# Layer-norm roots on GpSimd and a tile-by-tile opening in a fused attention and SwiGLU kernel

## The chip, the cores and the metric

The kernel runs on one core of a Trainium2 chip. The metric is the device time of one execution in microseconds; it was measured in three runs. The engines are TensorE (PE, with its weight loads as PEld), VectorE (DVE), ScalarE (ACT), GpSimd (POOL) and SyncE (SP, which here only issues transfers).

## What is computed

```
xn = layernorm(x)                                  # x: 2048 x 640, bf16
q  = (xn @ wq) in 32 heads of 192                  # wq: 640 x 6144
p  = softmax(q k^T / sqrt(192))                    # k, v: 32 heads x 2048 x 192
s  = (p v, heads side by side) @ wo                # wo: 6144 x 640
g  = silu( (silu(xn @ w1) * (xn @ w3)) @ w2 )      # w1, w3: 640 x 1536, w2: 1536 x 640
out = x + s * g
```

## The kernel before

**Tiling.** The 2048 rows of x are 16 tiles of 128. Four tiles are a chunk of 512 queries (`qb`). A *pass* is one head with one chunk; it goes over 8 pairs of key tiles (`p`). For each pair, PE computes transposed scores into one of two PSUM buffers (`scores`, tag `st2`), ScalarE takes the exponential (`weights`, L509), and PE multiplies the result with the values (`values`, L542) into two banks `ob0` and `ob1`, of which there is one each. At the end of a pass VectorE reads a bank (`evict`, L518), and only then may the next pass write it. Value products lag behind the scores: `advance` keeps them in the list `parts` and lets 12 to 16 of them stand.

**The bound.** The exponential subtracts a bound on the scores rather than their maximum. Its bias `nb` comes from largest absolute values of queries and keys, multiplied, summed over the partitions. For the first pass the sum is a product on PE (`first_bound`); for the later ones it is GpSimd's partition_all_reduce (`next_bound`, L450). That instruction is in a loadable library of GpSimd, which the kernel loads first of all (L73).

**The first passes.** Heads 0 and 1 go first, in the order (head 0, chunk 0), (1, 0), (0, 1), (0, 2), (0, 3), (1, 1), (1, 2), (1, 3), called passes 0 to 7. During them the rest of layer norm is done: `ln_stats` takes mean and variance of a tile on VectorE, `ln_root` its reciprocal root, `ln_scale` applies both on VectorE, and the tile is turned, on PE in the opening (`ln_turn`), later by a transposing DMA (`dma_turn`) into `xnT`. The tables `extras` and `posts` say after which pair of which pass each such step is issued; `late_project` projects a chunk of queries when its tiles are there. From head 2 on everything repeats evenly; then come the feed-forward part (`ffn_hidden`, `ffn_out`) and the output product.

**The opening.** PE runs filler products (`keep_busy`) until the first rows are normalised. Tiles 0 to 3 are counted on VectorE, tile 1 on ScalarE (`stats_on_scalar`). The root is exp(-0.5 ln(var + eps)) on ScalarE: two small activations for two tiles. All four tiles are scaled, then turned, then copied, and the queries of head 0 (`pq`) and the gate columns that ride along (`pf`) are projected in two halves of two tiles each.

**Order.** Nearly every instruction here is pinned: it stays on its engine in the order in which the code issues it. An instruction that waits therefore holds all behind it on that engine. GpSimd also makes the swapped copies of keys (`KS`, L154) and queries (`qS`, `qD`, L378, L384) on which scores wait.

Of the kernel before, what the change touches and what calls it, by code (L numbers as in the profile page):

```python
# [15 lines left out]
P = 128  # L16
DH = 192
# [13 lines left out]
def _kernel_impl(ctx, tc, A_x, A_k_cache, A_v_cache, A_wq, A_wo, B_w1, B_w3, B_w2, out):  # L31
# [36 lines left out]
    eps_t = const.tile([P, 1], F32, name="eps_t")  # L68
# [6 lines left out]
    pin(nc.vector.memset(eps_t[:], eps))  # L75
# [99 lines left out]
    with ExitStack() as actx:  # L175
# [20 lines left out]
        load_x(nc.sync, 0, 1)  # L196
        load_x(nc.scalar, 1, 2)
        load_x(nc.sync, 2, 3)
        load_x(nc.scalar, 3, 4)
        pin(nc.scalar.preload_act_table_set("natural_log_exp_and_others"))  # L200
        for load in first_loads[0]:
            load(nc.scalar)
        keys0 = new_keys()
        load_key_part(0, keys0, 0, HALF // 2, pin)

        def second_keys(behind):
            for load in first_loads[1]:
                load(nc.sync)
            second = load_key_part(0, keys0, HALF // 2, HALF, pin)
            tc.add_manual_dep(second.ins, behind.ins.name,  # L210
                              mybir.DependencyInfo(mybir.DependencyClass.Sync, mybir.DependencyReason.DATA),
                              reason="the first rows go ahead")

        fill = ps_o.tile([P, 2, 512], F32, tag="ob1", name="fill")
# [37 lines left out]
        def ln_turn(i, pool, tag, cp):  # L252
            pst = pool.tile([P, 2, 1024], BF16, tag=tag, name="pst")
            xn = scaled.pop(i)
            for c in range(DC):
                pin(nc.tensor.transpose(out=pst[:, 0, c * P:(c + 1) * P], in_=xn[:, c * P:(c + 1) * P], identity=ident_bf[:]))  # L256
            return lambda: pin(cp(out=xnT[:, i, :, :], in_=pst[:, 0, 0:D].rearrange("p (c q) -> p c q", c=DC)))
# [8 lines left out]
        def stats_on_scalar(i):  # L266
            xi, mean, var = x_all[:, i, :], mv[:, i, 0:1], mv[:, i, 1:2]
            total = lnp.tile([P, 2], F32, tag="total", name="total")
            spare = lnx.tile([P, D], BF16, name="spare")
            pin(nc.scalar.activation(out=spare[:], in_=xi, func=ACT.Identity, accum_out=total[:, 0:1]))  # L270
            pin(nc.scalar.mul(out=mean, in_=total[:, 0:1], mul=1.0 / D))

            def squares():
                pin(nc.scalar.activation(out=spare[:], in_=xi, func=ACT.Square, scale=-1.0, bias=mean,
                                         accum_out=total[:, 1:2]))
                pin(nc.scalar.mul(out=var, in_=total[:, 1:2], mul=1.0 / D))

            return squares

        keep_busy(11)  # L280
        squares = stats_on_scalar(1)
        squares()
        second_keys(ln_stats(0))
        values0 = kvp.tile([P, NKT, DH + 2], BF16, tag="vt", name="vt")
        load_values_part(0, values0, 0, 4, pin)
        load_x(nc.sync, 4, 6)
        keys1 = new_keys()
        load_key_part(1, keys1, 0, HALF // 2, pin)
        load_values_part(0, values0, 4, 8, pin)
        load_key_part(1, keys1, HALF // 2, HALF, pin)  # L290
        load_x(nc.sync, 6, 8)
        values1 = kvp.tile([P, NKT, DH + 2], BF16, tag="vt", name="vt")
        load_values_part(1, values1, 0, 4, pin)
        load_x(nc.sync, 8, 10)
        load_values_part(1, values1, 4, 8, pin)
        load_x(nc.sync, 10, 12)

        keep_busy(2, behind=ln_stats(2))
        ln_root(0)
        keep_busy(1, behind=ln_stats(3))  # L300
        ln_root(2)
        for i in range(4):
            ln_scale(i)
        turned = []
        for i in range(4):
            pool, tag = (ps_st, "st2") if i < 2 else (ps_o, f"ob{3 - i}")
            turned.append(ln_turn(i, pool, tag, (nc.scalar.copy, nc.vector.tensor_copy)[i % 2]))
        for step in turned:
            last_rows = step()
# [15 lines left out]

        def whole_product(out, w, qb, cs=range(DC), t0=0, t1=4):
            for c in cs:
                pin(nc.tensor.matmul(out[:, t0 * P:t1 * P], lhsT=w[:, c, :], rhs=rows_of(qb, c, t0=t0, t1=t1),  # L328
                                     start=(c == 0 and t0 == 0), stop=(c == DC - 1 and t1 == 4)))
# [104 lines left out]
        def first_bound(pr):  # L434
            bp = ps_o.tile([P, 2, 512], F32, tag="ob0", name="bp")
# [98 lines left out]
        def values(hd, qb, p, pT2, first):  # L534
# [14 lines left out]
            if p in (0, NPAIR - 1) and not first:  # L549
# [10 lines left out]
        def advance(hd, qb, p, extra=None, st2=None, hold=False):  # L560
# [12 lines left out]
            parts.extend(values(hd, qb, p, pT2, first))  # L573
# [4 lines left out]
            while len(parts) > (16 if p == 1 and (extra or hold) else 14 if extra or hold else 12):  # L578
# [8 lines left out]
        pq, pf = (ps_st.tile([P, 1024], F32, tag="st2", name=name) for name in ("pq", "pf"))  # L587
        for t0 in (0, 2):
            whole_product(pq[:, 0:512], first_ws[0][0], 0, t0=t0, t1=t0 + 2)
            whole_product(pf[:, 0:512], first_ws[0][1], 0, t0=t0, t1=t0 + 2)  # L590
        pin(nc.scalar.copy(out=heads[0]["qA"][:, 0:512], in_=pq[:, 0:512]))
        pin(nc.scalar.copy(out=heads[0]["qF"][:, 0:512], in_=pf[:, 0:512]))
# [4 lines left out]
        for swap in swap_rows(0, 0, nc.vector.tensor_copy):  # L597
# [6 lines left out]
        tc.add_manual_dep(key_copies[1]()[0].ins, multiplied.ins.name,  # L604
                          mybir.DependencyInfo(mybir.DependencyClass.Sync, mybir.DependencyReason.DATA),
                          reason="the first bound goes ahead")
        pa = ps_o.tile([P, 2, 512], F32, tag="ob0", name="pa")
        whole_product(pa[:, 0, :], first_ws[1][0], 0)
        pin(nc.scalar.copy(out=heads[1]["qA"][:, 0:512], in_=pa[:, 0, :]))
        pb = ps_o.tile([P, 2, 512], F32, tag="ob1", name="pb")  # L610
        whole_product(pb[:, 0, :], first_ws[1][1], 0, range(2))
        early = [scores(heads[0], 0, 0)]
        first_bound(pr)
        whole_product(pb[:, 0, :], first_ws[1][1], 0, range(2, DC))
        early.append(scores(heads[0], 0, 1))
        query_max(1, 0, 0)
        pin(nc.vector.tensor_copy(out=heads[1]["qF"][:, 0:512], in_=pb[:, 0, :]))
# [3 lines left out]
                          reason="the bound goes first")  # L621
        lower_rows(1, 0)
# [524 lines left out]
```

## Time and profile before

| | |
|---|---|
| time, median of 3 runs | 1934.91 us (1934.74 to 1935.07) |
| the profiled execution's own time | 1936.5 us |
| its span, first to last instruction | 1934.7 us |
| PE busy | 1927.1 us |
| ACT busy | 1275.9 us |
| DVE busy | 953.2 us |
| POOL busy | 446.1 us |
| granted TensorE clock | 1.000 |

The profile is of one execution. A row of the timeline gives start and length in microseconds, the engine and the line, the operation with `out<-in`, the size, and in brackets how long the engine sat idle before it and who ended that. Rows with a q behind the engine's name are its queue: issued transfers and other control work. The view by stretches gives for each stretch its length and then, for each engine, the busy time and the number of instructions.

### The profile page before, as it was taken

The numbers are of one execution on the slowest core, as the hardware profiler recorded it, in microseconds if no ns is written. First come the engines' busy times: TensorE is split into PE (matmuls) and PEld (weight loads), VectorE is DVE, ScalarE is ACT, GpSimd is POOL, SyncE is SP. The second block draws the span as 40 slices with busy tenths as digits, with TensorE's granted clock in tenths as the row PEclk, the third lists the DMA queues.
The fourth block names the chain that finished last, engine by engine and source line by source line (L and its number), as shares of the span: only waits on it lengthen the run. The fifth ranks groups of instructions, "written<-read, shape, count | busy, mean of one in ns | idle before, by whom it ended". The sixth has DMA issues, their size and how long they took to land.

```text
span 1934.7 us, 59549 instructions
## 1 busy us (share of the span) xinstructions
PE 1927.1 (100%) x26813; PEld 1297.3 (67%) x26813; DVE 953.2 (49%) x1804; ACT 1275.9 (66%) x1286; POOL 446.1 (23%) x755
## 2 busy tenths in 40 slices
PE   9999999999999999999999999999999999999999
PEld 6777766666666777766666666677776666445555
DVE  7765555554545554555555555555554544421111
ACT  7777777777777777777777777777777777210000
POOL 1532222222222222223222222222222210000000
PEclk9999999999999999999999999999999999999999
DMA  8422223131212222232422222213131102957662
GB/s 170 94 71 50 71 41 80 41 79 41 58 38 65 48 62 54 58 77 71 104 50 71 50 71 50 71 42 79 42 79 40 33 10 75 274 104 152 147 139 53
DMA packets 333285, 145.32 MB, mean 75 GB/s; under 512 B 284928, under 2 KB 326848, under 8 KB 333024
## 3 DMA queue, kind: packets, MB, share of 16 engines
q1 hardware_dynamic: 317392, 112.64, 25.3%
q0 software_dynamic: 7744, 23.60, 4.3%
q10 hardware_dynamic: 7888, 5.21, 0.9%
q8 instruction: 211, 3.46, 0.8%
q14 instruction: 50, 0.41, 0.1%
HBM read 56.23 MB, written 31.98 MB: 46 GB/s over the span
## 4 chain that ended last, share of the span: by engine, by line
PE 99%; DVE 0%; DMA 0%; issue 0%
PE obank L542 35%; PE st L502 34%; PE ps L344 14%; PE ps_s L875 7%; PE ps_f L928 2%; PE ps_t L884 2%; PE ps_gu L328 1%; PE ps_s L902 1%; PE ps_f L938 0%; PE ps_gu L344 0%; DMA xnT<-xn 0%; DVE osum L518 0%; DVE st L231 0%; DMA x_all<-in_A_x_dram 0%; PE pst L256 0%; PE ps_f L930 0%
## 5 line engine op out<-in xcount | busy, mean ns | idle before, releaser
L509 ACT ACTIVATE pT<-st,nb 128x1024 bf16<-128x1024 f32 x960 | 1068.2, 1113 | 328.4 <-PE st L502 324.2
L542 PEld LDWEIGHTS <-pT 64*128 64x128 bf16 x16384 | 723.4, 94 | 233.8 <-issue 1.2
L542 PE MATMUL obank<-vt,pT 64*128 64x193 bf16 x16384 | 858.0, 243 | 0.1
L518 DVE TENSOR_REDUCE osum<-obank 128x386 f32<-128x772 f32 x256 | 234.5, 957 | 639.9 <-PE obank L542 639.9
L502 PE MATMUL st<-qD,KT 64*128 64x512 bf16 x1024 | 385.4, 376 | 0.0
L502 PE MATMUL st<-qS,KS 64*128 64x512 bf16 x1024 | 385.3, 376 | 0.0
L502 PE MATMUL st<-qA,KT 64*128 64x512 bf16 x1024 | 385.2, 376 | 0.0
L502 PE MATMUL st<-qF,KT 64*128 64x512 bf16 x1024 | 385.2, 376 | 0.0
L502 PE MATMUL st<-qS,KT 64*128 64x512 bf16 x1024 | 385.2, 376 | 0.0
L502 PE MATMUL st<-qA,KS 64*128 64x512 bf16 x1024 | 385.0, 376 | 0.0
L502 PEld LDWEIGHTS <-KT 64*128 64x128 bf16 x4096 | 292.3, 94 | 131.7 <-issue 0.8
L344 PE MATMUL ps<-xnT,w 64*128 64x512 bf16 (+1 forms) x2540 | 314.6, 374 | 1.5 <-DMA xnT<-xn 1.5
L378 POOL COPY qS<-qA 64x512 bf16<-64x512 bf16 x254 | 158.0, 622 | 566.1 <-ACT qA L388 557.3
L344 PEld LDWEIGHTS <-w 64*128 64x128 bf16 x2540 | 127.6, 94 | 115.2 <-DMA xnT<-xn 1.7
L502 PEld LDWEIGHTS <-KS 64*128 64x128 bf16 x2048 | 174.5, 94 | 7.3 <-issue 0.2
L525 DVE TENSOR_TENSOR ostage<-osum,rl_all 128x384 bf16<-128x384 f32 x256 | 143.0, 559 | 8.9
L875 PE MATMUL ps_s<-wo_sb,oT 128*128 128x512 bf16 x672 | 146.2, 379 | 0.0
L154 POOL COPY KS<-KT 64x1024 bf16<-64x1024 bf16 (+1 forms) x68 | 68.2, 1003 | 235.0 <-DMA KT<-in_A_k_cache_dram 199.9
L108 POOL DMA_DIRECT2D w<-in_A_wq_dram x60 | 52.9, 882 | 289.9 <-PE ps L344 289.8
L389 DVE CAST qF<-ps 128x512 bf16<-128x512 f32 x120 | 83.0, 692 | 72.1 <-ACT qA L388 72.1
L875 PEld LDWEIGHTS <-oT 128*128 128x128 bf16 x672 | 65.7, 98 | 77.8
L372 DVE TENSOR_REDUCE st<-qA 128x1 f32<-128x512 bf16 (+1 forms) x130 | 87.4, 673 | 6.1 <-ACT qA L388 6.0
(112 smaller groups left out, 1109.7 us busy)
## 6 DMA issues: line engine op xcount, KB each, us to landing
o_scr<-ostage SPq DMA_DIRECT2D x64, 384.0 KB, 2.7
vt<-in_A_v_cache_dram SPq DMA_DIRECT2D x60, 384.0 KB, 5.0
wo_sb<-in_A_wo_dram POOLq DMA_DIRECT2D x1, 7680.0 KB, 32.4
w<-in_A_wq_dram POOLq DMA_DIRECT2D x30, 160.0 KB, 3.6
hT_scr<-hblk SPq DMA_DIRECT2D x16, 256.0 KB, 3.1
xt<-in_A_x_dram POOLq DMA_DIRECT2D x8, 320.0 KB, 3.4
w<-in_B_w_dram POOLq DMA_DIRECT2D x30, 80.0 KB, 2.6
w<-in_A_wq_dram POOLq DMA_DIRECT2D x30, 80.0 KB, 3.0
```

Source lines behind the costliest of these rows:

```text
L108: return lambda eng: keep(eng.dma_start(out=w[:, :, c0:c1], in_=src[:, s0:s0 + c1 - c0].rearrange("(c p) d -> p c d", p=P)))
L154: return [keep(nc.gpsimd.tensor_copy(out=KS[ROWS[r], c0:c1], in_=ks[ROWS[1 - r], 2 * r, c0:c1])) for r in range(2)]
L344: mm = pin(nc.tensor.matmul(out[:, t * 512 + t0 * P:t * 512 + (t0 + step) * P], lhsT=ws[t][ROWS[r], c, :], rhs=rows_of(qb, c, ROWS[r], t0, ...
L372: pin(nc.vector.tensor_reduce(out=hd["st"][r, 2 + s, qb:qb + 1], in_=src[r, qb * 512:qb * 512 + n], axis=AX.X, op=ALU.max, apply_absolute_ ...
L378: return [lambda t=t: keep(copy(out=hd["qS"][ROWS[t], qs], in_=hd["qA"][ROWS[1 - t], qs])) for t in range(2)]
L389: pin(cast(out=hd["qF"][:, qs], in_=ps[:, 512:1024]))
L502: pin(nc.tensor.matmul(st2[:, t * 512:(t + 1) * 512], lhsT=k[ROWS[t]], rhs=q[ROWS[t], qs], start=(s == 0), stop=(s == 2)))
L509: pin(nc.scalar.activation(out=pT2[:, c0:c1], in_=st2[:, c0:c1], func=ACT.Exp, scale=SCALE, bias=nb))
L518: pin(nc.vector.tensor_reduce(out=osum[:], in_=ob[:].rearrange("p t (j c) -> p j c t", j=2)[:, :, 0:DH + 1, :], axis=AX.X, op=ALU.add))
L525: pin(nc.vector.tensor_tensor(out=ostage[:, b * 2:b * 2 + 2, hg * DH:(hg + 1) * DH], in0=osum[:, :, 0:DH], in1=rl.unsqueeze(2).to_broadcas ...
L542: pin(nc.tensor.matmul(acc["o"][b][:, r, j * 256:j * 256 + DH + 1], lhsT=pT2[ROWS[r], t * 512 + i * P:t * 512 + (i + 1) * P], rhs=vt[ROWS[ ...
L875: pin(nc.tensor.matmul(ps, lhsT=oT[:, i % 2, k, :], rhs=wo_sb[:, k, 0:WIDE], start=(k == 0), stop=(k == OC - 1)))
```

## The change

Roots: variance plus eps, then a power of -0.5, two small instructions on GpSimd in the place of two on ScalarE. Ln is not used any more, so one table of ScalarE serves the kernel from the start, and the later table load (`tanh_table`) goes. The first four tiles have roots for tile 0, tiles 1 and 2, and tile 3; tile 0 is scaled before tile 3 is counted, and turned and multiplied before the others; the projection goes tile by tile. `pq` and `pf` share one buffer. Tiles 0 and 1 are loaded in halves by two queues. The weights of head 1 are loaded before any keys, and all keys behind tile 0's statistics. The second head's two products stand side by side in bank `ob0`, ahead of the first scores. In `posts`, tiles 6 and 7 get root, scaling and turning after pair 6 of pass 0 (before: in pass 1), and the second half of head 1's keys is copied there. In the first two passes the last value products are ordered bank by bank, and in passes 1 and 2 more of them are issued at pair 0. Behind the last head, the first hidden product is made in halves. `stats_on_scalar` needs one small activation less.

```
+    minus_half = const.tile([P, 4], F32, name="minus_half")
+    pin(nc.gpsimd.memset(minus_half[:], -0.5))
...
         def ln_root(i0, n=2):
-            lv = lnp.tile([P, 4], F32, tag="lv", name="lv")
-            pin(nc.scalar.activation(out=lv[:, 0:n].unsqueeze(2), in_=mv[:, i0:i0 + n, 1:2], func=ACT.Ln, bias=eps_t[:],
-                                     scale=1.0))
+            var = lnp.tile([P, 4], F32, tag="var", name="var")
+            pin(nc.gpsimd.tensor_scalar(out=var[:, 0:n].unsqueeze(2), in0=mv[:, i0:i0 + n, 1:2], scalar1=eps, scalar2=None,
+                                        op0=ALU.add))
             root = lnx.tile([P, 4], F32, name=f"rstd{i0}")
-            pin(nc.scalar.activation(out=root[:, 0:n], in_=lv[:, 0:n], func=ACT.Exp, scale=-0.5))
+            pin(nc.gpsimd.tensor_tensor(out=root[:, 0:n], in0=var[:, 0:n], in1=minus_half[:, 0:n], op=ALU.pow))
...
+        keep_busy(12)
+        stats_on_scalar(1)
+        seen = ln_stats(0)
+        other_loads(seen)
+        keep_busy(2, behind=seen)
+        ln_root(0, 1)
+        ln_stats(2)
+        ln_scale(0)
+        ln_root(1, 2)
+        ln_stats(3)
+        ln_root(3, 1)
+        for i in range(1, 4):
             ln_scale(i)
...
+        ln_turn(0, psts[0])
+        ln_copy(0, psts[0], nc.scalar.copy)
+        keep_busy(2)
+        whole_product(pq, first_ws[0][0], 0, t0=0, t1=1)
+        ln_turn(1, psts[1])
+        ln_copy(1, psts[1], nc.scalar.copy)
+        whole_product(pf, first_ws[0][1], 0, t0=0, t1=1)
+        for i in (2, 3):
+            ln_turn(i, psts[i])
+            last_rows = ln_copy(i, psts[i], nc.vector.tensor_copy)
+        for i in range(1, 4):
+            whole_product(pq, first_ws[0][0], 0, t0=i, t1=i + 1)
+            whole_product(pf, first_ws[0][1], 0, t0=i, t1=i + 1)
...
-            if p in (0, NPAIR - 1) and not first:
+            if p in (0, NPAIR - 1) and not first or (p == NPAIR - 2 and bank_first):
...
+            if p == NPAIR - 1 and bank_first:
+                parts[-12:-4] = parts[-8:-4] + parts[-12:-8]
...
-            while len(parts) > (16 if p == 1 and (extra or hold) else 14 if extra or hold else 12):
+            while len(parts) > (16 if p == 1 and (extra or hold) else 14 if extra or hold else 8 if banks_out else 12):
...
         extras = {
-            (1, 5): ((ln_root, 8, 4), (late_project, 0, 1)),
+            (1, 5): ((late_project, 0, 1),),
...
-            (3, 1): ((tanh_table,), (late_project, 1, 1)),
+            (3, 1): ((late_project, 1, 1),),
...
         posts = {
-            (0, 0): ((complete_second,),),
-            (0, 2): ((ln_root, 4), (scale_and_turn, 4), (scale_and_turn, 5), (first_key_maxima, 1)),
-            (0, 3): ((next_bound, 1, 0), (lambda: loads.pop("second half")(),)),
+            (0, 2): ((ln_root, 4), (scale_and_turn, 4), (scale_and_turn, 5), (complete_second,)),
+            (0, 3): ((first_key_maxima, 1), (next_bound, 1, 0)),
             (0, 5): ((ln_stats, 6), (ln_stats, 7)),
-            (1, 0): ((ln_root, 6),),
-            (1, 1): ((scale_and_turn, 6), (scale_and_turn, 7), (load_x, nc.sync, 12, 16)),
+            (0, 6): ((ln_root, 6), (scale_and_turn, 6), (scale_and_turn, 7), (lambda: loads.pop("second half")(),)),
+            (1, 1): ((load_x, nc.sync, 12, 16),),
...
-            (1, 5): ((scale_and_turn, 8), (scale_and_turn, 9), (scale_and_turn, 10), (scale_and_turn, 11)),
+            (1, 5): ((ln_root, 8, 4), (scale_and_turn, 8), (scale_and_turn, 9), (scale_and_turn, 10), (scale_and_turn, 11)),
```

Unchanged and spoken of below: `(2, 5): ((ln_root, 12, 4), (scale_and_turn, 12), (scale_and_turn, 13))` in `posts`, and the bounds, which are issued with the projections.

More of the change, by code (lines that the diff above doesn't have):

```diff
@@ L202, in _kernel_impl @@
+        for load in (*first_loads[0], first_loads[1][0]):
             load(nc.scalar)
[L203 to L210, printed above, removed]
-                              mybir.DependencyInfo(mybir.DependencyClass.Sync, mybir.DependencyReason.DATA),
-                              reason="the first rows go ahead")
@@ L292, in _kernel_impl @@
[L292 to L302, printed above, removed]
-            ln_scale(i)
[L304 to L307, printed above, removed]
@@ L558, in _kernel_impl, with advance @@
         seconds = []
[L560 removed]
+        def advance(hd, qb, p, extra=None, st2=None, hold=False, bank_first=False, banks_out=False):
             def drain_late():
```

125 lines of the change are left out of this document (61 added, 64 removed).

## The prediction

> **What bounds the kernel now.** I read the page's engine shares first, then busy time by stretches, then who waited for whom.
>
> ```profile
> span 1934.7 us, 59549 instructions
> PE 1927.1 (100%) x26813; PEld 1297.3 (67%) x26813; DVE 953.2 (49%) x1804; ACT 1275.9 (66%) x1286; POOL 446.1 (23%) x755
> ...
> 0.00:15.00 15.00, 12.64 (x94) 7.73 (x96) 10.50 (x33) 9.20 (x20) 3.17 (x12) 1.00 0.99 204
> ...
> 25.00:40.00 15.00, 13.46 (x223) 10.22 (x219) 9.97 (x26) 10.66 (x15) 1.61 (x3) 1.00 0.77 151
> ...
> 40.00:75.00 35.00, 34.93 (x520) 25.01 (x518) 27.73 (x63) 27.52 (x32) 12.17 (x23) 1.00 0.41 87
> ...
> 75.00:1400.00 1325.00, 1325.00 (x20440) 927.19 (x20438) 710.77 (x1326) 1011.76 (x994) 371.88 (x623) 1.00 0.25 61
> ...
> 1640.00:1650.00 10.00, 10.00 (x118) 5.90 (x113) 3.18 (x5) 4.86 (x6) 1.90 (x3) 1.00 0.19 51
> ...
> PE ps L344 <- DMA xnT<-xn: 1.5, 1, 1.5
> ```
>
> The first pair of numbers in a stretch is its length and PE's busy time. PE is the bound from end to end: no idle time at all from 75 to 1400, none at the turn to the feed-forward part (1640 to 1650), 0.07 us from 40 to 75. What can still be won lies in the opening (15.00 - 12.64 = 2.36 us idle, and the filler products) and in 25 to 40, where 1.54 us are idle, 1.5 of them one wait for turned rows. What can be lost is not bounded so: anything that PE has to wait for adds its whole length.
>
> **The change: library loads on GpSimd.** The kernel picks a GpSimd library for partition_all_reduce and loads it at the start (L73). In the changed kernel's instruction order the new GpSimd instructions (an add of eps, then a power) have a different library: a load stands ahead of the first root, and the libraries then alternate. After the one of L73 there are six loads: roots; the bound of pass 1; the root of tiles 6 and 7; the bound of pass 2; the root of tiles 12 to 15; the bound of head 1's second chunk. None of these six is in the kernel before. What one costs, call it S, is the term that decides. Rows for it, from the view of one line, the timeline and the list of DMAs (last column: us from issue to landing; the last row belongs to the key transpose above it):
>
> ```profile
> L73 POOLq MODIFY_POOL_CONFIG  x2: 11/11/11, 0.8 to 0.9; - x2
> ...
> 0.92 0.15 POOL L163 MEMSET st<- 128x16 f32 x2 [0.46 <-POOLq L1131]
> ...
> x_all<-in_A_x_dram SPq DMA_DIRECT2D x2, 160.0 KB, 3.4
> ...
> L127 SPq DMA_TRANSPOSE KT<-in_A_k_cache_dram x1: 2664/2664/2664, 1.7 to 1.7; - x1
> ...
> DMA to landing us min/median/max: 7.3/7.3/7.3
> ```
>
> The lower end is L73 itself: two records of 11 ns, a memset right behind them at 0.92, so 0.02 us. But the kernel before only ever uses this one library; it may still be there from the execution before, and then nothing was loaded. A load that brings code has to fetch it, and the nearest rows are the fetches of the same opening: 3.4 us for a tile of rows, 7.3 us for the first keys, under the same DMA load (share 0.99). I take S = 7.3, the slowest of them, since all these loads run beside the densest traffic of the kernel; the range keeps 0.02 and 3.4. [...]
>
> **Opening.** The timeline holds the steps (start, us, engine, line); the landing row belongs to the key transpose issued at 5.99.
>
> ```profile
> 5.99 3.25 SPq L127 DMA_TRANSPOSE KT<-in_A_k_cache_dram  x1
> ...
> DMA to landing us min/median/max: 5.1/5.1/5.1
> ...
> 5.92 0.83 DVE L231 BATCH_NORM_STATS2 st<-x_all 128x6 f32<-128x320 bf16 x2
> ...
> 6.92 1.51 DVE L249 TENSOR_SCALAR xn<-x_all,mv,rstd 128x640 bf16<-128x640 bf16 x4
> ...
> 7.42 1.52 PE L256 MATMUL pst<-ident_bf,xn 128*128 128x128 bf16 x20
> ...
> 8.35 1.12 DVE L257 COPY xnT<-pst 128x640 bf16<-128x640 bf16 x2
> ...
> 9.39 0.68 DVE L411 TENSOR_REDUCE st<-KT 128x1 f32<-128x512 bf16 x1
> ...
> 10.81 0.58 ACT L591 CAST qA<-pq 128x512 bf16<-128x512 f32 x1 [1.50 <-PE pq L328]
> ...
> 11.43 0.61 DVE L378 COPY qS<-qA 64x512 bf16<-64x512 bf16 x2 [1.37 <-ACT qA L591]
> ...
> 13.95 3.44 ACT L509 ACTIVATE pT<-st,nb_all 128x256 bf16<-128x256 f32 x5 [0.75 <-DVE nb_all L439]
> ...
> 38.31 0.39 POOL L450 PARTITION_ALL_REDUCE nb_all<-ns  x1 [0.37 <-DVE ns L447]
> ...
> 74.28 0.18 POOL L417 COPY st<-km 64x2 f32<-64x2 f32 x1
> 74.50 0.18 POOL L418 COPY st<-km 64x2 f32<-64x2 f32 x1
> ```
>
> The load is issued behind the memsets, at about 1.2, and done at 1.2 + 7.3 = 8.5. A root is two small GpSimd instructions: 0.22 us apart at least (74.28 to 74.50), 0.39 at most (the row of an all-reduce); 0.3 each is taken, 0.6 for a root. Tile 0's root is there at 9.1; before, tile 0 is scaled from 6.92. VectorE now has the scaling of tile 0 (1.51/4 = 0.38) ahead of tile 3's statistics (5.92 to the scaling at 6.92, 1.0 us), so it holds them back: 9.5, then 10.5, root of tile 3 at 11.1, while tiles 1 and 2 are scaled. From there tile by tile: scale 0.38, turn 1.52/4 = 0.38, copy 0.56, five products of 128 columns at 0.075 (1.52/20) 0.38, and some 0.25 of handovers: 13.05 for the cast of qA, against 10.81. The rest of the chain to the first exponential is as long as before: **+2.3 us**.
>
> Three things are moved here at no price under that cover. Head 0's first keys are issued at about 6.0 instead of 1.7 (SP's queue puts head 1's gate weights and the wait for tile 0's statistics ahead); the second half of the keys was issued at that place (5.99) and landed 5.1 us on, so 11.1, before 13.05. Without the cover their maximum (0.68 us) would push the swaps from 11.43 to 11.8: +0.4. One more weight load goes through ScalarE's queue, ahead of rows that it has to wait for anyway. The halved row loads can shift the rows by some tenths either way; the library is later.
>
> **Pass 0 to pass 1.** A pass is one head by one chunk of 512 rows. The timeline again, in order of its engines; the landing row is that of the turned rows xnT.
>
> ```profile
> 16.82 1.27 POOL L154 COPY KS<-KT 64x512 bf16<-64x512 bf16 x2
> ...
> 24.88 1.95 DVE L518 TENSOR_REDUCE osum<-obank 128x386 f32<-128x772 f32 x2 [0.82 <-PE obank L542]
> ...
> 26.75 0.80 DVE L249 TENSOR_SCALAR xn<-x_all,mv,rstd 128x640 bf16<-128x640 bf16 x2
> ...
> 26.31 1.42 PE L542 MATMUL obank<-vt,pT 64*128 64x193 bf16 x24
> ...
> 31.33 0.72 PE L344 MATMUL ps<-xnT,w 64*128 64x256 bf16 x10
> ...
> 33.52 0.72 PE L344 MATMUL ps<-xnT,w 64*128 64x256 bf16 x10 [1.47 <-DMA xnT<-xn]
> ...
> DMA to landing us min/median/max: 2.6/2.6/6.0
> ```
>
> GpSimd copies head 1's keys until 18.09 now; with a root (0.6) ahead and 2.3 later it is 21.0. Then the load for the all-reduce: 28.3, all-reduce (0.39) 28.7. Then the load for the root of tiles 6 and 7: 36.0, root 36.6. This root is new on the path of PE: the diff moves it, and the scaling of tiles 6 and 7, ahead of pass 0's evictions (24.88), and VectorE runs in order. Scaling 0.80, first eviction 0.97: bank 0 is free at 38.4. PE's first value product of pass 1, at 26.31 before, so wanted at 28.6, starts there: **+9.8**. The second bank is free 0.97 later, its products would start after 0.33: some **+0.4** net of the like wait now. PE has nothing else queued: the scores behind stand in program order.
>
> One wait goes in return, the 1.47 us at 33.52: tiles 6 and 7 are scaled at 37.4 and land 2.6 to 6.0 later, by 43.4, and the projection now comes at 31.33 + 12.5 = 43.8: **-1.5**. Lag so far 11.0.
>
> **Pass 1 to 2, pass 2 to 3.** The same view, later:
>
> ```profile
> 36.67 1.28 POOL L378 COPY qS<-qA 64x512 bf16<-64x512 bf16 x2 [14.82 <-ACT qA L388]
> ...
> 38.98 3.41 ACT L509 ACTIVATE pT<-st,nb_all 128x1024 bf16<-128x1024 f32 x3 [0.37 <-PE st L502]
> ...
> 40.27 0.38 PE L502 MATMUL st<-qA,KT 64*128 64x512 bf16 x1
> ...
> 50.40 0.48 POOL L450 PARTITION_ALL_REDUCE nb_all<-ns  x1
> ...
> 50.05 1.51 DVE L249 TENSOR_SCALAR xn<-x_all,mv,rstd 128x640 bf16<-128x640 bf16 x4
> ...
> 53.18 1.83 DVE L518 TENSOR_REDUCE osum<-obank 128x386 f32<-128x772 f32 x2 [1.61 <-PE obank L542]
> ...
> 56.10 1.19 PE L542 MATMUL obank<-vt,pT 64*128 64x193 bf16 x24
> ```
>
> The bound of pass 2 has no slack now: all-reduce done at 38.70, its exponential at 38.98, PE's scores that reuse the buffer at 40.27, as that exponential ends. With the lag the copies end at 48.95; load until 56.25, all-reduce 56.65, exponential 56.9 instead of 50.0: **+6.9**.
>
> In the clock of before, the all-reduce at 50.40 ends at 50.88. The root of tiles 12 to 15 stands behind it: load 58.2, root 58.8, the four scalings 60.3, the first eviction (0.92) 61.2, which PE's first value product of pass 3 at 56.10 waits for: **+5.1**, and **+0.6** for bank 1. The sixth load (for head 1's second chunk) I cost at nothing: its bound is first used two passes on, and only the next chunk's copies, a projection later, are queued behind it on GpSimd.
>
> **The rest.** The eviction order and the freed banks can win at most the 0.1 us that 25 to 75 leaves beside the 1.47; the table load and the Ln/Exp pairs taken off ScalarE were beside a busy PE: nothing. The half products at the end replace 10 products of a PE that has no idle slice there: nothing either way beyond 0.1.
>
> Sum: 2.3 + 9.8 + 0.4 - 1.5 + 6.9 + 5.1 + 0.6 = **23.6 us**. The profiled execution took 1936.5, 1.6 above the median; 1960.1 against it, and 1934.9 + 23.6 = **1958.5** against the median. S counts about five times (once in the opening, twice into pass 1, once each into 2 and 3): 5 us for each us of S. At S = 3.4 the opening is bounded by the keys (+0.4), the steps give 2.4 - 1.5 + 3.0 + 1.8, together 6.1: 1941.0.
>
> **Rivals.**
> *Not slower: the loads cost nothing, as at L73.* For it: the only row that shows such a load, 0.02 us, and the memset behind it at once. Against it: there the library may have been resident. Then the keys set the opening (+0.4), the wait of 1.5 goes, the banks give 0.1: 1933.7. It decides below S of about 2.5, where the steps above add up to less than 3.9. To be faster by over 0.2% (3.9 us; I use this as what a measurement of this kernel can tell from no change) the opening would also have to give up most of its 2.36.
> *Two loads in a row in the opening.* If L73's load is real once two libraries alternate, the root's load starts 7.3 later: 1965.8. Against it: the last library used is that of L73 in both kernels, and its memset did not wait.
> *Only the exponential waits.* If evictions went ahead of the late scalings, only bounds would cost: 2.3 + about 2 + 6.9 - 1.5 = 9.7, 1944.6. The order on VectorE speaks against it; this lies in my range.
>
> **Chances.** Forecast, with S from 3.4 to about 9.5: 0.63, its own range 1941 to 1970; two loads 0.10; only the exponential 0.04; free loads 0.23, of which 0.18 within 0.2% and 0.05 faster. Slower 0.77. To hold 8 in 10 the range has to reach into the free case: 1932 to 1970.
>
> **What would show it.** Right: GpSimd's first power some 7 us after the second pair of pool-config records; the first exponential at about 16; an idle PE of 7 to 10 us before pass 1's first value products with VectorE's eviction behind a scaling; an exponential of pass 2 waiting for GpSimd. Wrong: the all-reduces still within 1 us of their sums, and no new wait on GpSimd: then S is nothing, and the time is near 1934.

## The result and the profile after

The changed kernel takes **1970.38 us** (median of 6 runs, 1969.33 to 1972.93); the kernel before, on the same chip, 1934.99 (1934.74 to 1936.33). The ratio is **1.0183** (95% interval 1.0172 to 1.0194): 35.4 us slower. The forecast was 1958.5, with a range of 1932 to 1970. The profiled execution took 1972.93 with a span of 1971.2; against the span of before, 1934.7, that is 36.5 more, all of it in the first 100 us: behind them TensorE is busy without a gap to 1400, as before.

The loads first, from the view of one line (ns min/median/max, first and last start) of the changed kernel. Its lines have moved: L249 and L252 are the root, L458 the all-reduce, L260 the scaling, L526 the eviction, L550 the value products, L517 the exponential.

```profile
L249 POOLq MODIFY_POOL_CONFIG  x6: 3/82/83, 1.1 to 79.0; - x6
...
L458 POOLq MODIFY_POOL_CONFIG  x6: 3/4/4, 28.3 to 89.6; - x6
```

L73, one load, has two records, so these are three loads of each library. The records themselves last nanoseconds. What a load costs is the idle time in brackets ahead of the first instruction of its library. The timeline of the changed kernel (start, us, engine; idle time and what ended it in brackets), in order of its engines:

```profile
8.04 0.25 POOL L249 TENSOR_SCALAR var<-mv 128x1 f32<-128x1 f32 x1 [6.93 <-DVE mv L243]
8.38 0.60 POOL L252 TENSOR_TENSOR rstd<-var,minus_half 128x1 f32<-128x1 f32 x1
...
34.13 0.40 POOL L458 PARTITION_ALL_REDUCE nb_all<-ns  x1 [6.03 <-issue]
41.66 0.24 POOL L249 TENSOR_SCALAR var<-mv 128x2 f32<-128x2 f32 x1 [7.13 <-issue]
...
64.16 0.40 POOL L458 PARTITION_ALL_REDUCE nb_all<-ns  x1 [6.12 <-DVE ostage L533]
...
86.00 0.25 POOL L249 TENSOR_SCALAR var<-mv 128x4 f32<-128x4 f32 x1 [6.98 <-issue]
...
9.01 0.45 DVE L260 TENSOR_SCALAR xn<-x_all,mv,rstd 128x640 bf16<-128x640 bf16 x1 [1.68 <-POOL rstd L252]
...
42.76 1.47 DVE L260 TENSOR_SCALAR xn<-x_all,mv,rstd 128x640 bf16<-128x640 bf16 x2 [11.81 <-POOL rstd L252]
44.15 1.81 DVE L526 TENSOR_REDUCE osum<-obank 128x386 f32<-128x772 f32 x2
...
87.43 2.47 DVE L260 TENSOR_SCALAR xn<-x_all,mv,rstd 128x640 bf16<-128x640 bf16 x4 [9.19 <-POOL rstd L252]
...
9.52 0.45 PE L266 MATMUL pst_a<-ident_bf,xn 128*128 128x128 bf16 x5 [4.13 <-DVE xn L260]
...
14.11 3.27 PE L289 MATMUL pqf<-xnT,w 128*128 128x128 bf16 x30
...
19.80 1.24 PE L289 MATMUL pab<-xnT,w 128*128 128x512 bf16 x5 [1.34 <-ACT qA L613]
...
45.15 2.35 PE L550 MATMUL obank<-vt,pT 64*128 64x193 bf16 x24 [8.60 <-DVE osum L526]
...
90.82 1.54 PE L550 MATMUL obank<-vt,pT 64*128 64x193 bf16 x14 [6.32 <-DVE osum L526]
...
17.42 0.58 ACT L597 CAST qA<-pqf 128x512 bf16<-128x512 f32 x1 [4.72 <-PE pqf L289]
...
22.16 4.62 ACT L517 ACTIVATE pT<-st,nb_all 128x256 bf16<-128x256 f32 x6 [0.50 <-DVE nb_all L447]
...
64.59 2.12 ACT L517 ACTIVATE pT<-st,nb_all 128x1024 bf16<-128x1024 f32 x2 [5.89 <-POOL nb_all L458]
```

The middle chain reads off as it was drawn before the run: all-reduce at 34.13, a load, the root at 41.66, the scaling of tiles 6 and 7 at 42.76, only then the eviction at 44.15, and PE, idle for 8.60, starts pass 1's value products at 45.15 instead of 26.31. What was not drawn stands in the granted clock (PEclk, the third number from the end) of the changed kernel, which was 1.00 in every stretch before:

```profile
12.00:16.00 4.00, 3.42 (x33) 3.26 (x32) 1.76 (x4) 0.69 (x1) 0.96 (x2) 0.50 1.21 286
...
44.00:48.00 4.00, 2.81 (x28) 2.18 (x29) 3.93 (x10) 0.00 (x0) 0.05 (x1) 0.50 0.53 96
48.00:52.00 4.00, 4.00 (x44) 2.84 (x42) 2.37 (x8) 1.66 (x2) 1.28 (x2) 0.59 0.45 154
...
68.00:72.00 4.00, 4.00 (x42) 3.02 (x38) 0.00 (x0) 1.54 (x2) 0.00 (x0) 0.53 0.00 0
...
92.00:96.00 4.00, 4.00 (x43) 3.04 (x38) 3.90 (x10) 1.11 (x1) 0.40 (x1) 0.55 0.64 128
```

Behind each of its three long waits in the passes (8.60, 5.12 and 6.32 us) TensorE works at half speed, from 45.15, 65.76 and 90.82 to 51.2, 71.7 and 95.6, where finer stretches show the clock at 1.00 again: 6.1, 6.0 and 4.8 us of slow work.

### The profile page after: what moved, and what is told of

Read it like the earlier page. It is cut to its first block, busy times and chain, and to the rows that moved or that the text cites. A ratio compares the mean times of both kernels' runs of the same rounds, so it can differ in the third digit from the quotient of the medians.

```text
span 1971.2 us, 59620 instructions
## 1 busy us (share of the span) xinstructions
PE 1937.0 (98%) x26823; PEld 1295.7 (66%) x26847; DVE 954.4 (48%) x1802; ACT 1272.9 (65%) x1273; POOL 454.2 (23%) x770
## 3 DMA queue, kind: packets, MB, share of 16 engines
q8 instruction: 211, 3.46, 0.7%
## 4 chain that ended last, share of the span: by engine, by line
PE 97%; issue 1%; DVE 1%; POOL 1%; ACT 0%; DMA 0%; SPq 0%; POOLq 0%; ACTq 0%
PE obank L550 35%; PE st L510 33%; PE ps L352 14%; PE ps_s L876 7%; PE ps_f L929 2%; PE ps_t L885 2%; PE ps_s L903 1%; PE ps_gu L289 1%; PE ps_gu L352 1%; PE ps_f L939 0%; DVE xn L260 0%; PE pqf L289 0%; DMA x_all<-in_A_x_dram 0%; DVE osum L526 0%; POOL rstd L252 0%
## 5 line engine op out<-in xcount | busy, mean ns | idle before, releaser
L517 ACT ACTIVATE pT<-st,nb 128x1024 bf16<-128x1024 f32 x960 | 1068.5, 1113 | 327.7 <-PE st L510 323.4
L550 PEld LDWEIGHTS <-pT 64*128 64x128 bf16 x16384 | 722.3, 94 | 255.6 <-issue 18.6
L550 PE MATMUL obank<-vt,pT 64*128 64x193 bf16 x16384 | 859.9, 244 | 15.0 <-DVE osum L526 14.9
L526 DVE TENSOR_REDUCE osum<-obank 128x386 f32<-128x772 f32 x256 | 234.2, 956 | 636.1 <-PE obank L550 636.0
L517 ACT ACTIVATE pT<-st,nb_all 128x1024 bf16<-128x1024 f32 (+2 forms) x66 | 71.1, 1087 | 53.7 <-PE st L510 44.6
```

The source lines that it names most:

```text
L517: pin(nc.scalar.activation(out=pT2[:, c0:c1], in_=st2[:, c0:c1], func=ACT.Exp, scale=SCALE, bias=nb))
L526: pin(nc.vector.tensor_reduce(out=osum[:], in_=ob[:].rearrange("p t (j c) -> p j c t", j=2)[:, :, 0:DH + 1, :], axis=AX.X, op=ALU.add))
L550: pin(nc.tensor.matmul(acc["o"][b][:, r, j * 256:j * 256 + DH + 1], lhsT=pT2[ROWS[r], t * 512 + i * P:t * 512 + (i + 1) * P], rhs=vt[ROWS[ ...
```

## The experiments

Two theories stood against each other. One: the library loads, and the slow clock behind the waits that they make, are the whole loss. The other: the new order is slow by itself. Neither is the whole: each holds in a part of the kernel.

| experiment | time, us | ratio to before, 95% interval |
|---|---|---|
| 1 the change, roots on ScalarE | 1941.58 | 1.0033, 1.0021 to 1.0046 |
| 2 before, roots on GpSimd | 1966.98 | 1.0166, 1.0151 to 1.0182 |
| 3 the change, TensorE filled ahead of the first tile | 1969.24 | 1.0178, 1.0163 to 1.0194 |
| 4 the change, tiles 6 and 7 scaled later | 1967.05 | 1.0168, 1.0152 to 1.0183 |
| 5 the later edits alone, old opening, roots on ScalarE | 1936.05 | 1.0007, 0.9998 to 1.0016 |
| 6 as 1, tiles 0 and 1 in whole transfers | 1938.17 | 1.0019, 1.0010 to 1.0028 |
| 7 as 1, bound ahead of head 1's second product | 1938.66 | 1.0020, 1.0010 to 1.0029 |
| 8 as 1, TensorE filled | 1938.96 | 1.0021, 1.0012 to 1.0031 |
| 9 as 5, rows of tiles 6 and 7 issued sooner | 1934.09 | 0.9995, 0.9986 to 1.0004 |
| 10 as 1, with 6, 7 and (8 instead of 10 in the first place) 8 together | 1936.37 | 1.0007, 0.9998 to 1.0016 |
| 11 as 2, first keys issued later | 1967.71 | one run |

The kernel before took 1934.70 to 1934.88 beside them.

### 1. The roots back on ScalarE

```diff
-pin(nc.gpsimd.tensor_scalar(out=var..., in0=mv..., scalar1=eps, ...))
-pin(nc.gpsimd.tensor_tensor(out=root..., in0=var..., in1=minus_half..., op=ALU.pow))
+pin(nc.scalar.activation(out=lv..., in_=mv..., func=ACT.Ln, bias=eps_t[:], scale=1.0))
+pin(nc.scalar.activation(out=root..., in_=lv..., func=ACT.Exp, scale=-0.5))
```

The activation table for the logarithm, and the later switch to the other table, come back with them.

> The changed kernel with one thing put back: the inverse roots are computed on ScalarE again (logarithm and exponential, with the one table they need and its later switch), so GpSimd uses one library only. Everything else of the change stays: the tile-by-tile opening, the order of loads, the earlier scalings, the eviction order. Theory (library loads on GpSimd, and the slow TensorE clock behind the idle stretches that they make, are the whole loss): the idle stretches of TensorE of 4 us and more and the stretches at a granted clock near 0.5 are gone, first exponential at 13.5 to 15.5, first value product of pass 1 at 26 to 28, time 1933 to 1938 against 1935 for the kernel before. Rival A (the new order itself is slow: head 1's products ahead of the bound, keys issued behind the weights, scalings ahead of evictions): the time stays above 1945. Rival B (the new order is a gain that the loads cover up): below 1931.

It took 1941.58, between the theory's range and the rival's: 28.8 us of the 35.5 above before's 1934.84 are gone, 6.7 stay. So the loads, with what hangs on them, are four fifths of the loss, and neither theory alone has it. Its timeline:

```profile
8.51 0.45 PE L266 MATMUL pst_a<-ident_bf,xn 128*128 128x128 bf16 x5 [1.61 <-DVE xn L260]
...
10.68 0.69 PE L289 MATMUL pqf<-xnT,w 128*128 128x128 bf16 x5 [1.28 <-ACT xnT L269]
...
14.04 3.24 PE L289 MATMUL pqf<-xnT,w 128*128 128x128 bf16 x30
...
34.43 1.23 PE L550 MATMUL obank<-vt,pT 64*128 64x193 bf16 x24
...
6.26 0.89 DVE L242 BATCH_NORM_STATS2 st<-x_all 128x6 f32<-128x320 bf16 x2 [1.65 <-DMA x_all<-in_A_x_dram]
...
22.07 3.44 ACT L517 ACTIVATE pT<-st,nb_all 128x256 bf16<-128x256 f32 x5 [0.50 <-DVE nb_all L447]
```

The first exponential starts at 22.07, as late as in the changed kernel (22.16), without any load. Tile 0 is turned 1.0 us sooner here (8.51 against 9.52), and that time is lost again up to ScalarE's copy of it (9.95 against 10.01), which the root of tile 3 holds up. So the new order alone makes the opening 8 us late, and the load lies beside that. The passes are cured: 34.43 is 26.31 plus the opening's lag.

### 2. The roots on GpSimd, in the old order

```diff
-pin(nc.scalar.activation(out=lv..., func=ACT.Ln, ...))
-pin(nc.scalar.activation(out=root..., func=ACT.Exp, scale=-0.5))
+pin(nc.gpsimd.tensor_scalar(out=var..., ...))
+pin(nc.gpsimd.tensor_tensor(out=root..., ..., op=ALU.pow))
```

> The kernel before with one thing of the change alone: the inverse roots as powers on GpSimd, everything else in the old order. Theory (loads of 6 to 7 us each, in series with what waits): about 6 us of GpSimd idle ahead of each switch, first exponential at 16 to 18.5, the exponentials that follow an all-reduce wait for GpSimd, TensorE idle for 4 us and more ahead of pass 2 and pass 3, each with a granted clock near 0.5 behind it; time 1950 to 1968. The eviction ahead of pass 1 is not behind a scaling in this order, so less is lost there than the 18.8 us of the changed kernel. Rival A (the new order is what is slow): 1934 to 1940. Rival B (loads are paid but the old order hides most of them): 1940 to 1948.

1966.98, near the upper end of the theory's range: the loads alone, with the slow clock behind them, cost 32.1 us. In this order they do set the opening:

```profile
20.89 4.62 ACT L509 ACTIVATE pT<-st,nb_all 128x256 bf16<-128x256 f32 x6 [0.75 <-DVE nb_all L439]
...
11.47 0.24 POOL L238 TENSOR_SCALAR var<-mv 128x2 f32<-128x2 f32 x1 [10.36 <-issue]
```

The first exponential was expected by 18.5 and came at 20.89, because the first load ended 10.36 us behind the memsets instead of 6.9. 32.1 and 6.7 make 38.8, the two together cost 35.5. In the opening the losses lie beside each other (the first exponential comes 6.9 late here, 8.1 in experiment 1, 8.2 with both); in pass 1 the new order adds a wait, which experiment 4 takes out.

### 3. TensorE kept busy ahead of the first tile

```diff
-keep_busy(2, behind=seen)
+keep_busy(20, behind=seen)
```

> The changed kernel with 18 more pairs of dummy products behind tile 0's statistics, so that TensorE isn't idle for the 4.13 us ahead of its first transposes; nothing else changes, and the GpSimd load still ends at about 8. Theory (the idle stretch is what halves the granted clock in the stretch from 12 to 16): the granted clock there is 0.95 or more, the thirty 128-column products take 1.6 to 2.0 us where they took 3.27, the first exponential is 1.5 to 2.5 us earlier than 22.16, and the time is 1 to 2.5 us shorter than the changed kernel's 1970.4, so 1968 to 1969.4. Rival (the clock falls for another reason, such as the amount of work so far): clock and time as in the changed kernel within 0.5 us.

The clock was 1.00 from 8 to 16, and the same thirty products took 1.84:

```profile
13.94 1.84 PE L289 MATMUL pqf<-xnT,w 128*128 128x128 bf16 x30
...
20.55 4.62 ACT L517 ACTIVATE pT<-st,nb_all 128x256 bf16<-128x256 f32 x6 [0.50 <-DVE nb_all L447]
```

The first exponential came 1.61 us sooner. The median, 1969.24, is 1.1 shorter, as the theory has it, but the executions of the two kernels overlap (1968.44 to 1971.30 here, 1969.33 to 1972.93 there), so this rests on the trace. So here the clock fell from idleness (0.50 behind the wait of 4.13 us), and dummy products prevented it.

### 4. Tiles 6 and 7 scaled later

```diff
-(0, 6): ((ln_root, 6), (scale_and_turn, 6), (scale_and_turn, 7), ...),
+(1, 0): ((ln_root, 6),),
+(1, 1): ((scale_and_turn, 6), (scale_and_turn, 7), ...),
```

> The changed kernel with the root and the scaling of tiles 6 and 7 put back to where they stood, in pass 1, behind pass 0's evictions on VectorE; the roots stay on GpSimd. Theory (pass 1's first value products wait for evictions that stand behind these scalings, which wait for a GpSimd load): the eviction of pass 0 no longer waits, the first value product of pass 1 comes at 35 to 38 instead of 45.15; the turned rows of tiles 6 and 7 then land at 45 to 49, and the projection that needs them waits, so only a part is kept: 1962 to 1968. Rival A (the evictions wait for something else): first value product at 45 as before, time 1970 within 1. Rival B (the wait only moves to the turned rows): first value product at 35 to 38 and time 1969 to 1972.

1967.05, 3.3 less, inside the theory's range. The eviction no longer waits and pass 1's value products start at 34.97, but the projection then waits for the turned rows:

```profile
34.97 1.19 PE L550 MATMUL obank<-vt,pT 64*128 64x193 bf16 x24
...
46.98 1.25 PE L352 MATMUL ps<-xnT,w 64*128 64x256 bf16 x10 [6.50 <-DMA xnT<-xn]
```

The theory's step on VectorE's order is confirmed; most of the gain is given back at the next use of the same root. Of the 10.2 us by which the products come sooner, 1.4 are not this edit's: in this execution the clock was 0.87 from 12 to 16, and the first exponential came at 20.76.

### 5 and 9. The later edits without the new opening

Experiment 5 is the kernel before with the diff's edits behind the opening (posts, order of evictions, freed banks, half products at the end); experiment 9 also moves one load:

```diff
 load_x(nc.sync, 4, 6)
+load_x(nc.sync, 6, 8)
 ...
 load_key_part(1, keys1, HALF // 2, HALF, pin)
-load_x(nc.sync, 6, 8)
```

> The kernel before with all of the change except its opening and its roots: the eviction order and the banks released sooner, the late scalings ahead of the evictions, the roots of tiles 8 to 11 behind the product, the end's half products; the old opening and the roots on ScalarE stay. With scalar roots the changed kernel's first exponential came 8.1 us late (22.07 against 13.95) but its span was only 5.5 longer, so some 2.6 us came back behind the opening, 1.47 of it the wait for turned rows. Theory (that gain belongs to these edits, and the new opening alone loses): 1931.5 to 1933.5 against 1934.8, first exponential at 13.9 to 14.1, no wait for turned rows. Rival (the gain came only because a late opening left the transfers more time): the wait for turned rows is still there and the time is 1934.3 to 1936.

It missed: 1936.05, and the wait moved rather than went. The expectation counts on 2.6 us that came back in experiment 1, by the spans; but the profiled execution of before was itself 1.6 above its median, and by the medians 6.7 of the 8.1 us stayed. The timeline is of the slowest of this kernel's eleven executions (1938.16; the fastest took 1934.01):

```profile
26.63 1.81 PE L542 MATMUL obank<-vt,pT 64*128 64x193 bf16 x24 [2.00 <-ACT pT L509]
...
28.22 0.63 PE L502 MATMUL st<-qA,KT 64*128 64x512 bf16 x1
...
25.04 0.30 ACT L238 ACTIVATE lv<-mv,eps_t 128x2 f32<-128x2 f32 x1 [2.05 <-DVE mv L232]
...
22.88 0.89 DVE L231 BATCH_NORM_STATS2 st<-x_all 128x6 f32<-128x320 bf16 x2 [1.98 <-DMA x_all<-in_A_x_dram]
```

Read from the bottom up: the statistics of tiles 6 and 7 wait for their rows, the root of ScalarE for the statistics, and the exponentials queued behind that root keep TensorE for 2.00 us. The scores behind it take 0.63 instead of 0.38, and the clock is 0.89 in the stretch from 25 to 40, where experiment 9 has 1.00. In experiment 1 those rows were issued at 16.22, here at 19.07, and the late opening wanted them only at 28.27.

> The kernel of the old opening with the later edits (1936.05, scalar roots), with one transfer moved: the rows of tiles 6 and 7 are issued right behind those of tiles 4 and 5, ahead of head 1's keys, instead of behind them. There VectorE's statistics of tile 6 waited 1.98 us for these rows until 22.88, the root on ScalarE waited 2.05 for them, and the exponentials behind it made TensorE wait 2.00 us. Theory (these late rows ate the gain of the later edits): the root no longer waits, TensorE has no idle stretch over 0.5 us behind its first transposes, first exponential at 13.9 to 14.5, time 1931.5 to 1933.5, so faster than the kernel before (1934.7). Rival (head 1's keys, now later, are as late as the rows were): a wait of 1 to 2 us for head 1's bound takes their place, 1934.5 to 1936.5.

1934.09 (1933.80 to 1934.22 in 11 runs, against 1934.51 to 1936.47 in 21 of the kernel before): no wait of TensorE behind the opening is left, and the spread of experiment 5 is gone. The time is 0.6 above the theory's range all the same. It is the best version found, but the interval of its ratio, 0.9986 to 1.0004, does not exclude no change. The 2.4 us between the two profiled spans (1932.3, 1934.7) are not its gain: the profiled execution of before was itself 1.6 above its median. Of the 64 executions of before beside these experiments, 59 took less than 1935.4 us, the profiled one 1936.5; whether the 59 have its wait of 1.47 us for turned rows at all is not shown.

### 6, 7, 8 and 10. What makes the new opening slow

All four stand on experiment 1. Experiment 6 loads tiles 0 and 1 whole; 7 splits head 1's products; 8 raises `keep_busy(2, behind=seen)` to 10 and the `keep_busy(2)` behind the first turn to 6; 10 does all this, with 8 in the place of 10:

```diff
-for eng, r in ((nc.sync, ROWS[0]), (nc.scalar, ROWS[1])):          # 6
-    pin(eng.dma_start(out=x_all[r, i, :], ...))
+load_x(nc.sync, 0, 1); load_x(nc.scalar, 1, 2)
...
-pab = ps_o.tile([P, 2, 512], F32, tag="ob0", name="pab")           # 7
...
+pa = ...; whole_product(pa[:, 0, :], first_ws[1][0], 0); ...
+pb = ...; whole_product(pb[:, 0, :], first_ws[1][1], 0, range(2))
 early = [scores(heads[0], 0, 0)]
 first_bound(pr)
+whole_product(pb[:, 0, :], first_ws[1][1], 0, range(2, DC))
```

> The kernel of the first experiment (the change with scalar roots) with tiles 0 and 1 loaded in one transfer each, as before the change, instead of two halves each. Theory (the halves delay what VectorE and ScalarE wait for: statistics of the third and second tile began at 6.26 and 5.67 instead of 4.93 and 4.07): these begin 1.2 to 1.6 us sooner, first exponential at 20.3 to 21.3 instead of 22.07, time 0.7 to 1.7 below the first experiment's 1941.6. Rival (the chain of tile 0 sets the end and takes its turn from elsewhere): first exponential within 0.3 of 22.07, time within 0.5.

> The kernel of the first experiment with head 1's two products in two tiles again, and most of the second behind the first scores and the bound, as before the change. Theory (the wait of 1.34 us for the cast that reads the other half of the same tile, and 0.65 us of product ahead of the scores, lie on the path): no wait of TensorE for the cast, from qA's cast to the first exponential 3.0 to 3.3 instead of 4.75, first exponential at 19.9 to 20.6, time 1.3 to 2.2 below 1941.6. Rival (the bound's own chain on VectorE is as late): first exponential 21.5 or later, time within 0.6 of 1941.6.

> The kernel of the first experiment with 8 more pairs of dummy products ahead of the first transposes and 4 more behind them, so that TensorE's two idle stretches of 1.61 and 1.28 us are filled. There the clock fell to 0.50 in the stretch from 12 to 16 although no idle stretch was longer than 1.61 us. Theory (several short idle stretches in a row do it too): clock 0.95 or more from 8 to 20, the thirty 128-column products take 1.84 instead of 3.24 us, first exponential at 20.0 to 20.8, time 1.0 to 1.8 below 1941.6. Rival (the clock falls for something other than idleness here): clock and time as there, within 0.5.

They took 3.4, 2.9 and 2.6 us off 1941.58, each more than expected. In 6 (first two rows) the second statistics start at 4.81 instead of 6.26 and the first exponential comes 3.97 sooner; in its stretches TensorE's clock is 1.00, so the shorter wait also saved the clock. What each is worth can be told from its ten executions: eight had a mean clock of 1.000 and took 1937.95 to 1938.28, two had 0.998, as most of experiment 1 had, and took 1940.7. The clock is 2.6 of the 3.4 us, the rows themselves 0.9:

```profile
4.81 0.83 DVE L241 BATCH_NORM_STATS2 st<-x_all 128x6 f32<-128x320 bf16 x2
...
18.10 3.44 ACT L516 ACTIVATE pT<-st,nb_all 128x256 bf16<-128x256 f32 x5 [0.50 <-DVE nb_all L446]
```

In 7 the stretch from qA's cast to the exponential is 3.01 instead of 4.75, 1.74 shorter, as expected. The cast itself came 1.19 sooner, which is not this edit's: the second statistics started at 5.68 instead of 6.26, and the slow stretch of the clock came and ended sooner in this execution (0.53 from 8 to 12 and 0.61 from 12 to 16, against 0.77 and 0.50), so that the thirty products took 2.60:

```profile
16.13 0.58 ACT L597 CAST qA<-pqf 128x512 bf16<-128x512 f32 x1 [4.05 <-PE pqf L289]
...
19.14 3.44 ACT L517 ACTIVATE pT<-st,nb_all 128x256 bf16<-128x256 f32 x5 [0.67 <-DVE nb_all L447]
```

In 8 the clock from 12 to 16 is 1.00 where experiment 1 had 0.50, and the thirty products again take 1.84:

```profile
12.86 1.84 PE L289 MATMUL pqf<-xnT,w 128*128 128x128 bf16 x30
```

> The changed kernel with scalar roots and the three edits of the opening together: tiles 0 and 1 in whole transfers, head 1's second product behind the bound in a tile of its own, and dummy products that keep TensorE busy. Alone they took 3.4, 2.9 and 2.6 us off 1941.6. Theory (rows and fill share the clock's part of 1.5 us, the rest adds): first exponential at 15.0 to 16.5, clock 1.00, time 1934 to 1936.5. Rival (the tile-by-tile chain of copies between ScalarE and TensorE is itself too long): first exponential at 16.5 to 18, time 1936.5 to 1938.

Together 5.2 us, inside the theory's range, and not the 8.9 that the three make singly: each had regained some of the same clock. Counted once, it comes out: 2.6 for the clock (experiment 8), 0.9 for the rows, and 1.9 for the split (1938.96 in experiment 8 against 1936.86 and 1937.35 in the two executions of experiment 7 at a clock of 1.000) make 5.4. The first exponential:

```profile
16.29 3.44 ACT L516 ACTIVATE pT<-st,nb_all 128x256 bf16<-128x256 f32 x5 [0.68 <-DVE nb_all L446]
```

2.3 us behind the old opening's: that much is left for the chain that goes tile by tile, in which TensorE still waits 0.6 for the copy of the other half of `pst_b` and 0.4 for ScalarE's copy of tile 0. The old opening, all four tiles at a time, stays the better one: experiment 9, with it, is 2.3 us shorter.

### 11. The first keys behind the statistics

```diff
-load_key_part(0, keys0, 0, HALF // 2, pin)        # at 1.67
 def second_keys(behind):
     for load in first_loads[1]:
         load(nc.sync)
+    first = load_key_part(0, keys0, 0, HALF // 2, pin)      # waits for tile 0's statistics
```

> The kernel before with roots on GpSimd (the second experiment), with the transposing loads of head 0's first keys issued behind tile 0's statistics and head 1's weights, as in the changed kernel, instead of at 1.67. There GpSimd's first library load ended 10.4 us after the last instruction ahead of it, in the changed kernel 6.9. Theory A (the load takes longer beside the transposing transfers): first root's instruction at 8 to 9 instead of 11.47. Theory B (the difference is in when the load is started, which the statistics of tile 1 decide in that order): 11 to 12 again.

```profile
10.73 0.24 POOL L238 TENSOR_SCALAR var<-mv 128x2 f32<-128x2 f32 x1 [9.62 <-issue]
```

0.74 us sooner: neither theory's number, nearer to the second. Why the first load of a run ends 6.9 us behind the memsets in the new order and 9.6 to 10.4 in the old one stays open. The traces hold one hint: tile 0's statistics, which the first root reads, are done at 5.20 in experiment 2 and at 4.94 here, and from there to that instruction it is 6.27 and 5.79 us, where the loads for a root inside the passes of the two have 6.94 to 7.64. Against it, the sums that the all-reduce at 95.17 in the changed kernel reads were done only at 94.53, 4.9 behind its load's records (89.6), and that did not put off the load.

## Why the prediction was wrong, by its own steps

The direction and the passes' mechanism were right; the time missed by 11.9 us, just outside the range. The lag against before at eight marks shows where (start in the trace of before, then of the changed kernel):

| mark | before | after | lag | step | predicted step |
|---|---|---|---|---|---|
| first exponential | 13.95 | 22.16 | 8.2 | 8.2 | 2.3 |
| pass 1's first value product | 26.31 | 45.15 | 18.8 | 10.6 | 9.8 |
| qA cast of head 0's next chunk | 36.02 | 56.04 | 20.0 | 1.2 | -1.1 |
| exponential that waits for the bound of pass 2 | 38.98 | 64.59 | 25.6 | 5.6 | 6.9 |
| qA cast of the chunk after it | 47.74 | 75.97 | 28.2 | 2.6 | 0 |
| pass 3's first value product | 56.10 | 90.82 | 34.7 | 6.5 | 5.1 |
| fourth qA cast | 62.59 | 99.73 | 37.1 | 2.4 | 0.6 |
| end of the span | 1934.7 | 1971.2 | 36.5 | -0.6 | 0 |

**The loads and where they bite: right.** The three load steps make 22.7 against the 21.8 of the sum. S itself was over-sized: 6.9 to 7.1 for the roots' library, 5.8 to 6.1 for the sums', not 7.3; a root was under-sized, 0.94 for one column (from 8.04, the add, to 8.98, the end of a power of 0.60) and not 0.6. The scalings behind it were under-sized too: the two at 42.76 took 1.47 and the four at 87.43 took 2.47, where the sum has 0.80 and 1.51. GpSimd was copying beside them (42.79 to 44.04 and 87.46 to 89.36). The loads that are shorter and the rest that is longer nearly offset each other, which is luck. That L73 costs nothing held (a memset starts at 0.92 in the changed kernel too), and the rival of two loads in a row is out: the first root came 6.9 us behind the memsets.

**The order on VectorE: right.** Shown by experiment 4; the rival of the exponential alone is out. The wait for turned rows went, as said. The 0.4 and 0.6 for the second bank did not come: TensorE waits for VectorE's evictions only twice, for a first bank each time.

```profile
PE obank L550 <- DVE osum L526: 14.9, 2, 8.6
```

**The opening: wrong, 5.9 us.** The failed sentence is "The rest of the chain to the first exponential is as long as before", with "Three things are moved here at no price" and the rows shifted by "some tenths". Tile 0 was scaled at 9.01, forecast for 9.1; qA's cast came at 17.42, forecast for 13.05, and the exponential 4.74 behind it instead of 3.14. Experiments 1, 6, 7 and 8 show why: halved transfers hold back the statistics (6.20 in the changed kernel, 4.93 before), one tile `pab` for two products makes the second wait 1.34 us for the cast of the first, with the bound behind it, and the clock adds 1.6 (experiment 3). One term of the chain was also too small, whatever the clock: the sum has five products (0.38) behind the last turn, but thirty stand there in program order, and qA's cast comes behind all of them, 1.84 at full clock (experiment 3) and 3.27 here. The 2.3 were ascribed to the load; without any load the opening is as late.

**The clock: a term left out, about 7.7 us in the passes.** It is the excess of the three steps behind a long wait over the forecast without the second banks (-1.5, 0 and 0): 2.7, 2.6 and 2.4. The stretches give much the same: (1 - PEclk) times TensorE's busy time from 44 to 52, 64 to 72 and 88 to 96 makes 8.1. For the opening experiments 3 and 8 show it by taking it away; in the passes it is read from the rows, and no run took it away there. The prediction had found idle stretches of 7 to 10 us and did not ask what the engine does behind them.

5.9 for the opening, 0.9 for the load steps and 7.7 for the clock, less the 1.0 of the second banks and 0.6 that came back behind 100 us, make the 12.9 between 36.5 and 23.6.

**The rest: nearly right.** The later edits were put at 0.1 beside the wait for turned rows; experiment 9 is 0.8 below before, which its interval does not tell from nothing. The sixth load (5.80 us, ended at 95.17) held nobody up.

## What to carry to other kernels

Ask of each GpSimd instruction which library it needs: two that alternate cost 5.8 to 7.6 us at each switch inside the passes here, and what was queued behind paid on other engines too (waits of 11.81 us on VectorE, 8.60 on TensorE and 5.89 on ScalarE). When a step is costed as an idle TensorE, add the half-speed work behind it (4.8 to 6.1 us of it behind waits of 5.12 to 8.60 here), and where it can't be avoided fill it with dummy products (tried here in the opening only). Before an opening is split into smaller steps, look at what the halves share (a transfer's start, a tile with two owners): here the second statistics came 1.3 us later (6.20, 4.93 before) and a product waited 1.34 us for a cast, and those waits cost more than the overlap brought.

## What the runs showed of the hardware that was not expected

The clock also fell where no gap was long. In experiment 1 two gaps of 1.61 and 1.28 us, with 0.9 us of work between them, were followed by 0.50 from 12 to 16; gaps of 1.08 and 0.38 in the same place (experiment 8) and of 1.15 and 0.37 (the kernel before) left it at 1.00.

```profile
12.00:16.00 4.00, 3.42 (x34) 3.25 (x32) 1.57 (x3) 0.63 (x1) 1.11 (x2) 0.50 1.23 223
...
12.00:16.00 4.00, 3.19 (x40) 2.44 (x40) 2.16 (x6) 1.41 (x4) 1.21 (x2) 1.00 1.24 203
```

(Experiment 1, then experiment 8.) The trace of the changed kernel says how idle it was before each fall. There the clock fell to 0.50 at 10.29, 37.59, 64.90 and 88.79, for 6.83, 13.65, 6.83 and 6.83 us, and was at 1.00 between for 20.48, 13.65 and 17.07; each of these lengths is 2, 4, 5 or 6 times 3.41. In stretches of 3.41 us from 3.46 to 99.03, TensorE was busy for 0.77, 0.82, 0.00 and 0.00 us in the four that end with a fall, and for 1.93 or more in each other one at 1.00. Of those at 0.50, the four that end with a rise were busy throughout, the others for 2.64 or less. The kernel before, at 1.00 throughout, has 1.89 (from 3.97 to 7.38) as the least busy stretch of this length in its first 99.5 us. Why two of the ten executions of experiment 6 had 0.998 and eight 1.000 is not shown, since only one of the ten has a trace.

The two libraries did not load equally fast. Inside the passes of the changed kernel and experiments 2, 3 and 4 GpSimd was idle for 6.83 to 7.56 us ahead of a root's first instruction behind a load (eight loads) and for 5.77 to 6.79 ahead of the first all-reduce behind one (twelve loads).

In the changed kernel a scaling on VectorE (128x640 bf16) took 0.43 to 0.45 us with no GpSimd copy beside it (nine of them). Six took 0.73 to 0.82, each with GpSimd copying beside it for three quarters of its length or more; one with a copy beside 0.68 of its length, at 26.52, took 0.45.
